# A fused retention and mixture-of-experts kernel: where the closing additions of each batch are done

## The chip, the cores and the metric

The kernel runs on one core of a Trainium2 chip. The metric is the device time of one execution in microseconds (us), taken as the median of several runs. The core's engines work side by side, each through its own queue in order: PE (matrix products), DVE (vector), ACT (scalar functions), POOL (general), and SP, whose queue issues the DMA transfers.

## The reference, cut to what matters

Linear attention with decay gives 3072 tokens of 512 features (4 batches of 768), and a mixture of 4 experts is applied to each token, in float32:

```
for t in range(768):
    state = gamma * state + outer(k[t], v[t])
    y[t] = scale * q[t] @ state
x = y as (3072, 512)
p = domain_probs / sum(domain_probs)
out = sum over e of p[:, e] * (relu(x @ w1[e]) @ w2[e])      # w1[e]: 512 x 1024, w2[e]: 1024 x 512
```

## The kernel before, in words

**Seven products.** Both layers use Winograd's form of Strassen's scheme: a product of 2 x 2 blocks is made of seven products of blocks, numbered 1 to 7, and some additions. Each float32 operand is split in a high and a low part (`oh` and `ol` for the hidden values, `oh` by a copy on ACT, `ol` by a subtraction), and each product is three matrix products. One product of one half is six matmuls of 128 x 384.

**Rounds, steps, passes.** The hidden width is done in rounds of 256 columns, 16 rounds per batch (NRND), 64 in all. A round has seven steps (SEQ), each one product of layer 1 (p1, L483). The first batch uses another form of layer 2 (p2). From batch 1 on, layer 2 works on groups of two rounds, eight groups per batch (NP): each step does one unit of the group before, so that a group has 14 units, U0 to U13 below. `UNITS` (L43) gives their order: products 1, 3, 6, 7, 5, 4, 2, each for the half d = 0 and then d = 1 of 128 output columns. After the last round only units are left, 14 of them: the tail.

**A unit** (L553) multiplies into one of two PSUM banks, `ps_u`. In a batch's first group ACT copies the result to a tile `sum` in SBUF; afterwards DVE adds it to that tile (L420). The next unit but one needs the bank again, so PE cannot start it before this addition is done.

**Closing a batch.** After a unit of the eighth group, `finish` (L573) puts the last additions of Winograd's scheme, between tiles `sum` (L578), and the stores of the four result blocks (L584) on a list, `soon`, each with a wait: an entry with wait w is issued w + 1 passes later. `pass_step` (L477) runs once ahead of each step, 14 passes to a group. The order in which a queue gets its instructions is thus the order of the code and of these waits; an engine does not skip ahead. Before, POOL does most of the closing sums and DVE two per half, 3 + 6 and 3 + 5.

**Beside it** run, through the same queues: in each round, DVE's evacuations of layer 1 (`ps_y`, `ps_c`, `ps_z`, L420, and the gated values `b`, L454), four subtractions of POOL on `b` (L456, three together and one for product 4), ACT's copies `oh` (L442) and the subtractions `ol` (L447), on POOL for products 5, 7, 6 and 4, on DVE for 1, 3 and 2; and in the next batch's attention the products `ps_s` on PE and `sp` on DVE (L142), and the scaling of `kv` on POOL (L127). Batch 3 is the last, so there is no attention beside the closing of batch 2, nor beside the tail.

**Weights** of layer 1 are fetched four steps ahead (five buffers), those of layer 2 two pairs of units ahead (`v2`, three buffers, L323), all on SP's queue, which also issues the stores.

Of the kernel before, what the change touches and what calls it, by code (L numbers as in the profile page):

```python
# [12 lines left out]
B, H, S, D = 4, 8, 768, 64  # L13
# [12 lines left out]
NP = NRND // 2  # L26
# [14 lines left out]


UNITS = tuple((i, d) for i in (1, 3, 6, 7, 5, 4, 2) for d in range(2))  # L43
A2_AT = {1: 0, 2: 2, 4: 3, 6: 4, 7: 5, 3: 6, 5: 7}
LO_POOL = (5, 7, 6, 4)

# [4 lines left out]
def retention_moe(ctx: ExitStack, tc: tile.TileContext, qk, kv, w1, w2, probs, probt, cmask, cqs, cks, cys, out, out_t):  # L51
    nc = tc.nc
# [21 lines left out]
    def open_pool(name, bufs):  # L74
        npool[name] = sc_n.enter_context(tc.tile_pool(name=name, bufs=bufs, reuse_waits="tile"))
# [231 lines left out]

    wp1, wp2 = {}, {}

    def fetch_w1(g):  # L310

        n, k = divmod(g, 7)
        if NRND <= n < NRND * B:
            i = SEQ[k]
            wp1[n, i] = v1_p.tile([128, 2, 256], F32R, tag="v1", name="v1")
            nc.sync.dma_start(out=wp1[n, i].bitcast(F32), in_=kept1[n % NRND][:, A_AT[i]])

    def fetch_w2(g):
        q, k = divmod(g, 7)
        if q < NP * B:  # L320
            i = UNITS[2 * k][0]
            wp2[q, i] = npool["v2"].tile([128, 2, 2, 256], F32R, tag="v2", name="v2")
            nc.sync.dma_start(out=wp2[q, i].bitcast(F32), in_=kept2[q % NP][:, A2_AT[i]])  # L323

# [92 lines left out]
    def add(ps, u, o=None):  # L417

        o = ps if o is None else o
        nc.vector.tensor_tensor(out=o, in0=ps, in1=u, op=ALU.add)  # L420
        return o
# [129 lines left out]
    outs = []  # L551

    def unit(q, k):  # L553
        i, d = UNITS[k]
        b, qb = divmod(q, NP)
        w = wp2[q, i]
        ps = ps_o.tile([128, 512], F32, tag="o", name="ps_u")[:, 0:HB]
        ds = slice(128 * d, 128 * d + 128)
        m = 0
        for r in range(2):  # L560
            hi, lo, _ = op[2 * q + r, i]
            for l, o in ((0, hi), (0, lo), (1, hi)):
                nc.tensor.matmul(ps, lhsT=w[:, r, l, ds], rhs=o, start=(m == 0), stop=(m == 5))  # L563
                m += 1
        if qb == 0:
            psum[b, i, d] = npool["s"].tile([128, HB], F32, tag="ps", name="sum")
            nc.scalar.activation(out=psum[b, i, d], in_=ps, func=ACTF.Copy)
        else:
            add(ps, psum[b, i, d], psum[b, i, d])
        if qb == NP - 1:  # L570
            finish(b, i, d)

    def finish(b, i, d):  # L573
        p = {j: psum[b, j, d] for j in range(1, 8)}
        e1, e2 = nc.gpsimd, nc.vector

        def sums(wait, e, o, x):
            soon.append((wait, lambda: e.tensor_tensor(out=p[o], in0=p[o], in1=p[x], op=ALU.add)))  # L578

        def store(wait, j, f, h):  # L580

            rows = out_t[256 * f + 128 * d:256 * f + 128 * d + 128]
            to = rows[:, (b - 1) * S + HB * h:(b - 1) * S + HB * h + HB]
            soon.append((wait, lambda: nc.sync.dma_start(out=to, in_=p[j])))  # L584

        if i == 1:
            sums(0, e1, 2, 1)
        elif i == 6:
            sums(0, e1, 6, 1)
            sums(2, e2, 3, 6)  # L590
        elif i == 7:
            sums(0, e1, 7, 6)
            sums(1, e1, 4, 7)
        elif i == 5:
            sums(0, e1, 7, 5)
            sums(0, e2, 3, 5)
            store(2, 7, 1, 1)
            store(2, 3, 0, 1)
        elif i == 4:
            store(1, 4, 1, 0)  # L600
        elif i == 2:
            store(0, 2, 0, 0)


    def att_steps(b):
        ci0 = b * NCHB
        load_qk(ci0 + 1)
        for ci in range(ci0, ci0 + NCHB):
            old = ci > ci0
            last = ci == ci0 + NCHB - 1  # L610
            decay(ci)
            scale_v(ci)
            scores(ci)
            yield
            if old:
                values(ci - 1, not last)
                if ci - 1 >= ci0 + 3:
                    combine_x(b, ci - 1 - ci0 - 3, nc.vector, nc.gpsimd)
                load_qk(ci + 1)
            else:  # L620
                state(ci)()
            load_kv(ci + 1)
            yield
        values(ci, False)
        yield
        combine_x(b, 2, nc.vector, nc.gpsimd)
        yield

    with tc.manual_schedule():
# [65 lines left out]
        for n in range(NRND * B):  # L695
            g, r = divmod(n, NRND)
            if r == 0 and g + 1 < B:
                steps = att_steps(g + 1)
                due = -1.0
            if n == NRND:  # L700
                sc_a.close()
                open_pool("g", 2)
                open_pool("b", 6)
                fetch_gate(n)
            tiles = [3, 4, 5, 0, 1, 2] if 0 < n <= NRND else []
            q, first = divmod(n, 2)
            for k, i in enumerate(SEQ if n else FIRST):
                t = 7 * n + k
                fetch_w1(t + 4)
                pass_step()  # L710
                if n == NRND and k == 3:
                    for x in tiles:
                        p2(n - 1, x)
                    tiles = []
                    sc_b.close()
                    open_pool("op", 15)
                    open_pool("s", 14)
                    open_pool("v2", 3)
                if n > NRND and r % RPE == 0 and k == 0:
                    fetch_gate(n)  # L720
                s14 = 7 * first + k
                if n >= NRND and q == NRND // 2 and s14 == 10:
                    fetch_w2(7 * q)
                    fetch_w2(7 * q + 1)
                p1(n, i)
                if n > NRND + 1:
                    if s14 % 2 == 0:
                        fetch_w2(7 * (q - 1) + s14 // 2 + 2)
                    unit(q - 1, s14)
                elif k and tiles:  # L730
                    for _ in range(2 if n == NRND else 1):
                        p2(n - 1, tiles.pop(0))
                if r == NRND - 1 and g + 1 < B:
                    x_hi(g + 1, i)
                    e = nc.gpsimd if k in XPOOL else nc.vector
                    soon.append((XLATE[k] - 1 if g else 0, lambda b=g + 1, i=i, e=e: x_lo(b, i, eng=e)))
                if n < NRND:
                    weights(n, k)
                if n == NRND and k == 0:
                    save_w2(n - 1, wc2, 4)  # L740
                due += ATT_STEPS / 13 / 7
                while due >= 1 - 1e-6:
                    due -= 1
                    next(steps, None)
        q = NP * B - 1
# [64 lines left out]
```

## Time and profile before

| | |
|---|---|
| median of 3 runs (lowest, highest) | 1091.43 us (1091.34, 1093.07) |
| profiled execution, its own time | 1093.62 us |
| its span, first to last instruction | 1090.7 us |
| PE busy | 1050.8 us, 96% |
| DVE busy | 724.4 us, 66% |
| POOL busy | 679.6 us, 62% |
| ACT busy | 378.3 us, 35% |

The profile is of one execution. A line of its timeline gives start, length, engine, line of the code, operation, output <- inputs, and in brackets how long the engine had been idle and what ended that. Rows with x2 or more are merged, and their length is that of the whole. The length of an instruction can hold a wait for a port. The windows view gives busy time per engine in a stretch and the clock granted to PE, 1.00 being full speed.

### The profile page before, as it was taken

To read this page: it belongs to the slowest core of one execution; us is meant where nothing else is said; L and a number is where in the kernel's file an instruction comes from. 1 tells how busy PE (TensorE), PEld (TensorE's weight loads), DVE (VectorE), ACT (ScalarE), POOL (GpSimd) and SP (SyncE) were. 2 spreads that over 40 slices of the span, in tenths; PEclk is the share of its full clock that TensorE was granted. 3 is DMA by queue.
4 is the path that set the end of the run, shared out by engine and by line. 5 is a ranking of instruction groups with operands and counts; after the bars stand their busy time and mean duration, and the time that the engine had idled before them with its cause. 6 is when DMAs were issued, how large, how long until landed. Compare 5 with 4: busy or idle time off the path is not lost.

```text
span 1090.7 us, 18579 instructions
## 1 busy us (share of the span) xinstructions
PE 1050.8 (96%) x6696; PEld 993.4 (91%) x6696; DVE 724.4 (66%) x1214; ACT 378.3 (35%) x737; POOL 679.6 (62%) x645
## 2 busy tenths in 40 slices
PE   6689999999999999999999899999999899999996
PEld 5578888888878999999999899999999899999995
DVE  5857666676766476676688556667669546666665
ACT  2343433444443423223252432332233343333330
POOL 3566666666626656556579655656668865555557
PEclk9899999999999999999999999999999999999999
DMA  8479999999898888878786987877788788888875
GB/s 323 145 261 312 345 308 312 300 347 310 285 303 291 262 268 265 277 258 271 242 260 219 331 279 238 272 266 257 233 256 261 254 270 253 261 262 256 265 223 168
DMA packets 154603, 293.70 MB, mean 269 GB/s; under 512 B 12688, under 2 KB 77328, under 8 KB 154512
## 3 DMA queue, kind: packets, MB, share of 16 engines
q1 hardware_dynamic: 153792, 291.66, 81.9%
q8 instruction: 53, 0.87, 0.3%
q10 hardware_dynamic: 720, 0.86, 0.2%
q14 instruction: 38, 0.31, 0.1%
HBM read 223.22 MB, written 69.26 MB: 268 GB/s over the span
## 4 chain that ended last, share of the span: by engine, by line
PE 81%; DVE 7%; POOL 5%; DMA 3%; issue 2%; ACT 1%; SPq 0%; ACTq 0%; DVEq 0%; POOLq 0%
PE ps_u L563 28%; PE ps_x L502 22%; PE ps_o L537 11%; PE ps_z L502 11%; PE ps_y L502 5%; POOL b L456 2%; POOL sum L578 2%; PE ps_s L139 2%; PE ps_v L186 2%; DVE xl L240 2%; DVE ol L447 1%; POOL ol L447 1%; PE ps_v L180 1%; DMA w2r<-in_w 1%; DMA v<-k 1%
## 5 line engine op out<-in xcount | busy, mean ns | idle before, releaser
L563 PE MATMUL ps_u<-oh,v 128*128 128x384 f32 x1344 | 395.5, 336 | 8.5 <-DVE sum L420 8.5
L456 POOL TENSOR_TENSOR b<-b 128x384 f32<-128x384 f32 x192 | 206.7, 1076 | 179.0 <-DVE b L454 147.5
L563 PEld LDWEIGHTS ps_u<-oh,v 128*128 128x128 f32 x1344 | 247.8, 188 | 12.2 <-DVE sum L420 12.0
L447 POOL TENSOR_TENSOR ol<-b,oh 128x384 fp32r<-128x384 f32 x192 | 207.8, 1094 | 81.1 <-ACT oh L442 43.5
L420 DVE TENSOR_TENSOR sum<-ps_u,sum 128x384 f32<-128x384 f32 x294 | 161.7, 550 | 136.4 <-PE ps_u L563 129.0
L442 ACT ACTIVATE oh<-b 128x384 fp32r<-128x384 f32 x336 | 163.1, 520 | 214.5 <-POOL b L456 123.8
L502 PE MATMUL ps_x<-xh,v 128*128 128x384 f32 x768 | 227.2, 336 | 1.3 <-ACT u L414 1.3
L563 PE MATMUL ps_u<-ol,v 128*128 128x384 f32 x672 | 225.0, 335 | 1.3 <-POOL ol L447 1.3
L414 ACT ACTIVATE u<-ps_x 128x384 f32<-128x384 f32 x128 | 62.6, 489 | 238.5 <-PE ps_x L502 238.4
L502 PEld LDWEIGHTS ps_x<-xh,v 128*128 128x128 f32 x768 | 141.4, 188 | 3.4 <-ACT u L414 1.6
L447 DVE TENSOR_TENSOR ol<-b,oh 128x384 fp32r<-128x384 f32 x144 | 127.9, 888 | 22.2 <-ACT oh L442 22.1
L502 PE MATMUL ps_x<-xl,v 128*128 128x384 f32 x384 | 128.4, 334 | 0.0
L563 PEld LDWEIGHTS ps_u<-ol,v 128*128 128x128 f32 x672 | 126.3, 188 | 1.7 <-POOL ol L447 1.7
L502 PE MATMUL ps_z<-xh,v 128*128 128x384 f32 x384 | 115.0, 340 | 2.4 <-DMA v<-k 2.4
L545 DVE SCALAR_TENSOR_TENSOR acc<-ps_o,pm,acc 128x512 f32<-128x512 f32 x90 | 67.0, 745 | 54.9 <-PE ps_o L537 54.9
L537 PE MATMUL ps_o<-w2l,hh 128*128 128x512 f32 x192 | 76.6, 399 | 0.0
L537 PE MATMUL ps_o<-w2h,hh 128*128 128x512 f32 x192 | 76.5, 398 | 0.2
L537 PE MATMUL ps_o<-w2h,hl 128*128 128x512 f32 x192 | 76.5, 398 | 0.0
L502 PEld LDWEIGHTS ps_z<-xh,v 128*128 128x128 f32 x384 | 71.6, 190 | 3.8 <-DVE c2l L290 2.7
L502 PEld LDWEIGHTS ps_x<-xl,v 128*128 128x128 f32 x384 | 72.1, 188 | 0.1
L502 PE MATMUL ps_z<-xl,v 128*128 128x384 f32 x192 | 64.8, 338 | 0.0
L420 DVE TENSOR_TENSOR ps_y<-ps_y,u 128x384 f32<-128x384 f32 x64 | 36.0, 563 | 33.6 <-PE ps_y L502 33.6
(109 smaller groups left out, 1630.5 us busy)
## 6 DMA issues: line engine op xcount, KB each, us to landing
v<-k SPq DMA_DIRECT2D x336, 256.0 KB, 3.8
v<-k SPq DMA_DIRECT2D x168, 512.0 KB, 4.5
k<-w1h SPq DMA_DIRECT2D x16, 896.0 KB, 6.3
k<-w1l SPq DMA_DIRECT2D x16, 896.0 KB, 8.4
qk<-in_qk SPq DMA_DIRECT2D x24, 512.0 KB, 5.5
kv<-in_kv SPq DMA_DIRECT2D x23, 512.0 KB, 5.8
w1r<-in_w SPq DMA_DIRECT2D x16, 512.0 KB, 7.9
w2r<-in_w SPq DMA_DIRECT2D x16, 512.0 KB, 4.3
```

Source lines behind the costliest of these rows:

```text
L139: nc.tensor.matmul(ps[r][:, p, :], lhsT=a[rows, 1, p, :], rhs=a[rows, 0, p, :], start=True, stop=True)
L186: nc.tensor.matmul(ps[r][64 * k:64 * k + 64, half, :], lhsT=v[:, 1, h, :], rhs=sp[:, h, :], start=(c == 0 and half == 0), stop=True, skip_ ...
L240: eng.tensor_tensor(out=lo, in0=x_part(b, i, o), in1=hi.bitcast(F32), op=ALU.subtract)
L414: nc.scalar.activation(out=t, in_=ps, func=ACTF.Copy)
L420: nc.vector.tensor_tensor(out=o, in0=ps, in1=u, op=ALU.add)
L442: nc.scalar.activation(out=hi, in_=t, func=ACTF.Copy)
L447: eng.tensor_tensor(out=lo, in0=t, in1=hi.bitcast(F32), op=ALU.subtract)
L456: sub = lambda o, a, b: nc.gpsimd.tensor_tensor(out=o, in0=a, in1=b, op=ALU.subtract)
L502: nc.tensor.matmul(ps, lhsT=lhsT[:, cs], rhs=rhs[:, kt, :], start=(fresh and m == 0), stop=(m == 5), skip_group_check=True,)
L537: nc.tensor.matmul(ps, lhsT=a[:, ts], rhs=b[:, fs, :], start=(m == 0), stop=(m == 5))
L545: nc.vector.scalar_tensor_tensor(out=acc[nt], in0=ps, scalar=sc, in1=acc[nt], op0=ALU.mult, op1=ALU.add)
L563: nc.tensor.matmul(ps, lhsT=w[:, r, l, ds], rhs=o, start=(m == 0), stop=(m == 5))
```

## The change

Three things change. In batches 1 and 2 the closing sums get longer waits, and product 4's sum (4 + 7) goes from POOL to DVE and now follows the unit's own addition instead of preceding it; the last block is built as 5 + 7 in the tile of product 5 (before: 7 + 5, after 4 had taken 7). The stores move to later passes. In the tail (the closing of batch 3) the units have another order, products 1, 3, 5, 7, 6, 4, 2, and all sums of half 0 are on POOL, all of half 1 on DVE. The pool of `sum` tiles grows from 14 to 16 buffers.

```diff
+LAST_UNITS = tuple((i, d) for i in (1, 3, 5, 7, 6, 4, 2) for d in range(2))
...
+    def units(q):
+        return LAST_UNITS if q == NP * B - 1 else UNITS
...
     def finish(b, i, d):
         p = {j: psum[b, j, d] for j in range(1, 8)}
-        e1, e2 = nc.gpsimd, nc.vector
+        pool, dve = nc.gpsimd, nc.vector
...
-        if i == 1:
-            sums(0, e1, 2, 1)
+        if b == B - 1:
+            e = (pool, dve)[d]
+            if i == 1:
+                sums(1, e, 2, 1)
+            elif i == 5:
+                sums(1, e, 3, 5)
+            elif i == 6:
+                sums(0, e, 6, 1)
+                sums(0, e, 7, 6)
+                sums(0, e, 3, 6)
+                store(0, 3, 0, 1)
+                sums(0, e, 5, 7)
+                store(0, 5, 1, 1)
+            elif i == 4:
+                sums(0, e, 4, 7)
+                store(0, 4, 1, 0)
+            elif i == 2:
+                store(0, 2, 0, 0)
+        elif i == 1:
+            sums(4, pool, 2, 1)
         elif i == 6:
-            sums(0, e1, 6, 1)
-            sums(2, e2, 3, 6)
+            sums(1, pool, 6, 1)
+            sums(4, dve, 3, 6)
         elif i == 7:
-            sums(0, e1, 7, 6)
-            sums(1, e1, 4, 7)
+            sums(1, pool, 7, 6)
         elif i == 5:
-            sums(0, e1, 7, 5)
-            sums(0, e2, 3, 5)
-            store(2, 7, 1, 1)
-            store(2, 3, 0, 1)
+            sums(1, dve, 3, 5)
+            store(3, 3, 0, 1)
+            sums(3, pool, 5, 7)
+            store(5, 5, 1, 1)
         elif i == 4:
-            store(1, 4, 1, 0)
+            sums(2, dve, 4, 7)
+            store(4, 4, 1, 0)
         elif i == 2:
-            store(0, 2, 0, 0)
+            store(1, 2, 0, 0)
...
-                    open_pool("s", 14)
+                    open_pool("s", 16)
```

In the orders below the numbers of the tiles tell them apart. POOL at the closing of batch 1, from the first sum on product 7 on; product 7's sums are 3707 and 3730 (halves 0 and 1), product 6's 3648 and 3673, product 5's 3759 and 3787, product 4's 3811 and 3838. Before:

```order
L578 TENSOR_TENSOR sum_3707<-sum_3707,sum_3648 128x384
L447 TENSOR_TENSOR ol_6450<-b_6337,oh_6449 128x384
L578 TENSOR_TENSOR sum_3811<-sum_3811,sum_3707 128x384
L578 TENSOR_TENSOR sum_3730<-sum_3730,sum_3673 128x384
L447 TENSOR_TENSOR ol_6481<-b_6391,oh_6480 128x384
L447 TENSOR_TENSOR ol_6484<-b_6364,oh_6483 128x384
L578 TENSOR_TENSOR sum_3838<-sum_3838,sum_3730 128x384
L578 TENSOR_TENSOR sum_3707<-sum_3707,sum_3759 128x384
L456 TENSOR_TENSOR b_6411<-b_6411,b_6364 128x384
L578 TENSOR_TENSOR sum_3730<-sum_3730,sum_3787 128x384
L447 TENSOR_TENSOR ol_6536<-b_6411,oh_6535 128x384
L127 TENSOR_TENSOR kv_5526<-kv_5526,ks_113 128x512
```

The same stretch in the change:

```order
L582 TENSOR_TENSOR sum_3673<-sum_3673,sum_3567 128x384
L451 TENSOR_TENSOR ol_6448<-b_6335,oh_6447 128x384
L582 TENSOR_TENSOR sum_3707<-sum_3707,sum_3648 128x384
L451 TENSOR_TENSOR ol_6478<-b_6389,oh_6477 128x384
L451 TENSOR_TENSOR ol_6481<-b_6362,oh_6480 128x384
L582 TENSOR_TENSOR sum_3730<-sum_3730,sum_3673 128x384
L460 TENSOR_TENSOR b_6410<-b_6410,b_6362 128x384
L451 TENSOR_TENSOR ol_6531<-b_6410,oh_6530 128x384
L582 TENSOR_TENSOR sum_3759<-sum_3759,sum_3707 128x384
L128 TENSOR_TENSOR kv_5526<-kv_5526,ks_113 128x512
L582 TENSOR_TENSOR sum_3787<-sum_3787,sum_3730 128x384
```

Ahead of the single subtraction (b_6411, now b_6410) three sums have gone from this queue: the two of product 4 and the first with product 5, which now comes after it.

DVE at the end of the same closing, from the addition of U10 (sum_3811, product 4, half 0) on; sum_3880 and sum_3900 are U12 and U13. Before:

```order
L420 TENSOR_TENSOR sum_3811<-ps_u_6525,sum_3811 128x384
L420 TENSOR_TENSOR ps_c_6549<-ps_x_6430,u_6466 128x384
L454 SCALAR_TENSOR_TENSOR b_6551<-ps_c_6549,g_6246 128x384
L420 TENSOR_TENSOR sum_3838<-ps_u_6553,sum_3838 128x384
L447 TENSOR_TENSOR ol_6541<-b_6521,oh_6540 128x384
L420 TENSOR_TENSOR ps_z_6459<-ps_z_6459,u_6498 128x384
L454 SCALAR_TENSOR_TENSOR b_6578<-ps_z_6459,g_6246 128x384
L420 TENSOR_TENSOR sum_3880<-ps_u_6582,sum_3880 128x384
L142 TENSOR_TENSOR sp_6593<-ps_s_6594,mask_111 128x4x128
L447 TENSOR_TENSOR ol_6569<-b_6551,oh_6568 128x384
L454 SCALAR_TENSOR_TENSOR b_6617<-ps_x_6430,g_6246 128x384
L420 TENSOR_TENSOR sum_3900<-ps_u_6619,sum_3900 128x384
```

The change, from the sum that now follows U10's addition (the second sp is left out here as above):

```order
L582 TENSOR_TENSOR sum_3619<-sum_3619,sum_3787 128x384
L424 TENSOR_TENSOR ps_c_6543<-ps_x_6428,u_6462 128x384
L458 SCALAR_TENSOR_TENSOR b_6545<-ps_c_6543,g_6246 128x384
L424 TENSOR_TENSOR sum_3838<-ps_u_6547,sum_3838 128x384
L451 TENSOR_TENSOR ol_6535<-b_6516,oh_6534 128x384
L424 TENSOR_TENSOR ps_z_6455<-ps_z_6455,u_6493 128x384
L458 SCALAR_TENSOR_TENSOR b_6571<-ps_z_6455,g_6246 128x384
L424 TENSOR_TENSOR sum_3880<-ps_u_6575,sum_3880 128x384
L582 TENSOR_TENSOR sum_3811<-sum_3811,sum_3707 128x384
L451 TENSOR_TENSOR ol_6562<-b_6545,oh_6561 128x384
L458 SCALAR_TENSOR_TENSOR b_6611<-ps_x_6428,g_6246 128x384
L424 TENSOR_TENSOR sum_3900<-ps_u_6613,sum_3900 128x384
```

One of DVE's sums now stands behind U10's addition, and one (4 + 7) between the additions of U12 and U13. The three sums ahead of U10's (3 + 6 twice, 3 + 5) stand behind the additions of U8 and U9; before, all four stood between the additions of U6 and of U10.

DVE in the tail; product 6, half 1 is sum_9875, and product 4's halves are sum_10001 and sum_10028. Before, from the addition of U5 on:

```order
L420 TENSOR_TENSOR sum_9875<-ps_u_12212,sum_9875 128x384
L420 TENSOR_TENSOR sum_9897<-ps_u_12223,sum_9897 128x384
L578 TENSOR_TENSOR sum_9799<-sum_9799,sum_9850 128x384
L420 TENSOR_TENSOR sum_9920<-ps_u_12233,sum_9920 128x384
L578 TENSOR_TENSOR sum_9821<-sum_9821,sum_9875 128x384
L420 TENSOR_TENSOR sum_9949<-ps_u_12246,sum_9949 128x384
L578 TENSOR_TENSOR sum_9799<-sum_9799,sum_9949 128x384
L420 TENSOR_TENSOR sum_9977<-ps_u_12257,sum_9977 128x384
L578 TENSOR_TENSOR sum_9821<-sum_9821,sum_9977 128x384
L420 TENSOR_TENSOR sum_10001<-ps_u_12267,sum_10001 128x384
```

The change, from the addition of U9 (product 6, half 1) to the end:

```order
L424 TENSOR_TENSOR sum_9875<-ps_u_12255,sum_9875 128x384
L582 TENSOR_TENSOR sum_9875<-sum_9875,sum_9768 128x384
L582 TENSOR_TENSOR sum_9920<-sum_9920,sum_9875 128x384
L582 TENSOR_TENSOR sum_9821<-sum_9821,sum_9875 128x384
L582 TENSOR_TENSOR sum_9977<-sum_9977,sum_9920 128x384
L424 TENSOR_TENSOR sum_10001<-ps_u_12269,sum_10001 128x384
L424 TENSOR_TENSOR sum_10028<-ps_u_12279,sum_10028 128x384
L582 TENSOR_TENSOR sum_10028<-sum_10028,sum_9920 128x384
L424 TENSOR_TENSOR sum_10055<-ps_u_12289,sum_10055 128x384
L424 TENSOR_TENSOR sum_10075<-ps_u_12298,sum_10075 128x384
```

Four sums in a row now stand between the additions of U9 and U10, where before sums and additions alternated. POOL has five sums of half 0 in a row from the unit of product 6 on, besides 2 + 1 and 3 + 5 earlier.

More of the change, by code (lines that the diff above doesn't have):

```diff
@@ L320, in fetch_w2 @@
         if q < NP * B:
-            i = UNITS[2 * k][0]
+            i = units(q)[2 * k][0]
             wp2[q, i] = npool["v2"].tile([128, 2, 2, 256], F32R, tag="v2", name="v2")
@@ L553, in unit @@
     def unit(q, k):
-        i, d = UNITS[k]
+        i, d = units(q)[k]
         b, qb = divmod(q, NP)
```

## The prediction

> **What bounds the kernel now.** Read first: the page, then the windows view (columns: microseconds; busy PE, weight loads, DVE, ACT, POOL; clock; DMA).
>
> ```profile
> span 1090.7 us, 18579 instructions
> 600.00:650.00 50.00, 46.95 (x311) 45.30 (x310) 28.40 (x50) 20.22 (x45) 29.66 (x29) 1.00 0.91 307
> 650.00:700.00 50.00, 50.00 (x342) 48.77 (x341) 34.06 (x61) 14.12 (x30) 29.91 (x30) 1.00 0.79 254
> 850.00:900.00 50.00, 46.52 (x257) 45.88 (x257) 23.53 (x39) 20.63 (x46) 33.87 (x34) 0.97 0.80 265
> ```
>
> In the steady stretch PE is never idle. It idles where a batch closes: batch 1 around 600 us, batch 2 around 858, and in the tail. The timeline of PE has the gaps, in brackets with what ended them:
>
> ```profile
> 584.32 0.44 PE L563 MATMUL ps_u<-oh,v 128*128 128x384 f32 x1 [0.22 <-DVE sum L420]
> 602.79 0.44 PE L563 MATMUL ps_u<-oh,v 128*128 128x384 f32 x1 [2.31 <-DVE sum L420]
> 605.91 0.44 PE L563 MATMUL ps_u<-oh,v 128*128 128x384 f32 x1 [0.74 <-DVE sum L420]
> 842.42 0.44 PE L563 MATMUL ps_u<-oh,v 128*128 128x384 f32 x1 [0.21 <-DVE sum L420]
> 855.85 0.44 PE L563 MATMUL ps_u<-oh,v 128*128 128x384 f32 x1 [0.65 <-DVE sum L420]
> 861.06 0.51 PE L563 MATMUL ps_u<-oh,v 128*128 128x384 f32 x1 [2.83 <-DVE sum L420]
> 1072.12 0.45 PE L563 MATMUL ps_u<-ol,v 128*128 128x384 f32 x1 [1.34 <-POOL ol L447]
> 1078.51 0.44 PE L563 MATMUL ps_u<-oh,v 128*128 128x384 f32 x1 [1.59 <-DVE sum L420]
> ```
>
> Batch 1 loses 0.22 + 2.31 + 0.74 = 3.27 us, batch 2 loses 0.21 + 0.65 + 2.83 = 3.69. Nearly always a unit waits for the addition that empties the PSUM bank of the unit two before it. Batch 2 pays more: after the gap the clock is low.
>
> ```profile
> 861.00:865.00 4.00, 3.94 (x14) 3.94 (x15) 2.48 (x5) 1.31 (x3) 3.70 (x4) 0.57 0.95 264
> 318.21 0.41 PE L502 MATMUL ps_z<-xh,v 128*128 128x384 f32 x1 [2.41 <-DMA v<-k]
> 320.00:324.00 4.00, 4.00 (x15) 3.26 (x14) 1.26 (x3) 0.49 (x1) 0.00 (x0) 0.75 1.01 365
> 864.81 0.34 PE L563 MATMUL ps_u<-oh,v 128*128 128x384 f32 x1
> 1066.78 0.56 DVE L420 TENSOR_TENSOR sum<-ps_u,sum 128x384 f32<-128x384 f32 x1 [0.48 <-PE ps_u L563]
> 1067.82 0.56 DVE L420 TENSOR_TENSOR sum<-ps_u,sum 128x384 f32<-128x384 f32 x1 [0.48 <-PE ps_u L563]
> ```
>
> Undisturbed, a group of six matmuls takes 1.04 us: so far apart are the additions of the tail's first units, at 1066.78 and 1067.82, each waiting for PE. From 861.06 to 864.81 two groups take 3.75 us instead of 2.08: 1.67 more, so batch 2 costs 5.36. A gap of 2.41 us was followed by a low clock too, the one of 2.31 was not (clock 1.00 in the first window above).
>
> Why is the addition late? The rows around 600 us, on POOL, ACT and DVE:
>
> ```profile
> 595.93 1.95 POOL L578 TENSOR_TENSOR sum<-sum 128x384 f32<-128x384 f32 x2
> 597.84 0.99 POOL L456 TENSOR_TENSOR b<-b 128x384 f32<-128x384 f32 x1
> 598.87 1.35 ACT L442 ACTIVATE oh<-b 128x384 fp32r<-128x384 f32 x3 [8.77 <-POOL b L456]
> 596.95 0.56 DVE L420 TENSOR_TENSOR sum<-ps_u,sum 128x384 f32<-128x384 f32 x1 [2.18 <-POOL sum L578]
> 599.84 1.36 DVE L447 TENSOR_TENSOR ol<-b,oh 128x384 fp32r<-128x384 f32 x1 [2.34 <-ACT oh L442]
> 602.19 0.55 DVE L420 TENSOR_TENSOR sum<-ps_u,sum 128x384 f32<-128x384 f32 x1
> ```
>
> POOL's closing sums hold up its subtraction b (product 4 of the round before); ACT, in order, waits 8.77 us for it; DVE waits 2.18 us for a POOL sum, then 2.34 us for ACT; the addition of U12 ends at 602.74, and the next group's first unit starts at 602.79.
>
> **The change part by part: batches 1 and 2.** POOL loses the sums of product 4 and takes two for product 5 in place of the two on product 7. Of the old nine sums ahead of that subtraction six stay.
>
> ```profile
> L578 POOL TENSOR_TENSOR sum<-sum x30: 987/1026/1733, 573.9 to 1083.6; 128x384 f32<-128x384 f32 x30
> L578 DVE TENSOR_TENSOR sum<-sum x12: 547/890/1415, 585.6 to 1081.0; 128x384 f32<-128x384 f32 x12
> ```
>
> Three times 1.03 us brings its end from 598.83 to 595.7, and ACT's two copies (about 1.0) free DVE's ol at 596.7. The additions of products 4 no longer wait for POOL, since 4 + 7 now follows them on DVE: the 2.18 us wait goes. What is late next is DVE itself. In its new order, between the addition of U8 and that of U13, stand eight operations with two SBUF inputs (five sums, three ol), twelve that read PSUM, and the two sp. Their cadence:
>
> ```profile
> 592.09 0.55 DVE L420 TENSOR_TENSOR ps_y<-ps_y,u 128x384 f32<-128x384 f32 x1
> 594.21 0.56 DVE L454 SCALAR_TENSOR_TENSOR b<-ps_c,g 128x384 f32<-128x384 f32 x1
> 602.65 1.27 DVE L142 TENSOR_TENSOR sp<-ps_s,mask 128x512 f32<-128x512 f32 x2
> 586.53 0.33 PE L563 MATMUL ps_u<-oh,v 128*128 128x384 f32 x1
> 599.27 0.33 PE L502 MATMUL ps_x<-xh,v 128*128 128x384 f32 x1
> ```
>
> Four PSUM readers take 2.12 us from start to start, 0.53 each. U8 began at 586.53; without the gap of 0.22 and its slow restart (0.12) it begins at 586.19, and its addition is over at 587.9. With x for an operation with two SBUF inputs, the addition of U13 ends at 587.9 + 12 x 0.53 + 1.27 + 8x = 595.5 + 8x. The second unit of the next group needs it: from 599.27, less 0.34, plus 1.04 for the layer-1 product in between and 2.08 for one step, it is due at 602.05. So PE waits 8x - 6.5 us. x lies between 0.55 (alone) and 1.42; I take 1.0, somewhat above the median of the sums, 0.89, as POOL is busy throughout. The wait is 1.5 us, against 3.27: a gain of 1.8. At 0.55 nothing is left to wait for, a gain of 3.3; at 1.35 the wait is 4.3, a loss of 1.0. Here ol would start, at x = 1.0, at 587.9 + 5 + 7 x 0.53 = 596.6, just as POOL and ACT allow.
>
> Batch 2 has neither the sp on DVE nor the attention's matmuls on PE, which weigh alike (1.27 us, and 1.3: from 586.53 to 599.27 PE does eleven groups of 1.04 and these), so again 1.5 us, and no low clock: 5.36 - 1.5, a gain of 3.9 (5.4 down to -0.6).
>
> The stores go to later passes on SP's queue, past loads of weights that in before were issued behind them:
>
> ```profile
> 597.90 0.81 SPq L584 DMA_DIRECT2D out<-sum  x2
> ```
>
> The first store of batch 1 is issued at 597.90, just after POOL's sums at 595.93, and holds back the loads behind it; still none of the gaps above is ended by a DMA, as weights of layer 1 are fetched four steps (8.3 us) ahead. With sums ready about when their stores come up this gets easier, and it costs nothing; if a sum is late, the same 8.3 us cover it. Two more buffers of sums cover the later stores: nothing.
>
> **The tail.** Order 1, 3, 5, 7, 6, 4, 2: the units of 5 and 7 come before those of 6, as POOL makes their ol first, so the gap of 1.34 goes. Then one engine sums each half, both at once. That they hinder each other shows at 574 us, where DVE does two such operations in a row beside POOL:
>
> ```profile
> 573.94 1.73 POOL L578 TENSOR_TENSOR sum<-sum 128x384 f32<-128x384 f32 x1
> 573.50 1.30 DVE L240 TENSOR_TENSOR xl<-xr,xh 128x768 fp32r<-128x768 f32 x1
> 574.72 1.36 DVE L447 TENSOR_TENSOR ol<-b,oh 128x384 fp32r<-128x384 f32 x1
> 1075.61 9.03 POOL L578 TENSOR_TENSOR sum<-sum 128x384 f32<-128x384 f32 x8
> 1079.76 0.78 DVE L578 TENSOR_TENSOR sum<-sum 128x384 f32<-128x384 f32 x1
> 1081.05 0.78 DVE L578 TENSOR_TENSOR sum<-sum 128x384 f32<-128x384 f32 x1
> 1083.70 3.95 SPq L584 DMA_DIRECT2D out<-sum  x8
> v<-k SPq DMA_DIRECT2D x6, 512.0 KB, 3.9
> ```
>
> POOL's sum takes 1.73 instead of 1.03, ends at 575.67, and DVE's ol, started at 574.72, ends 0.41 later: they take turns. In the old tail DVE's sums beside POOL's ended 1.29 us apart. The Trainium skill, SBUF — State Buffer, section "SBUF: two separate sides", says so: VectorE and GpSimd share a port pair under an exclusive lock, held for an instruction, and a VectorE operation with two SBUF inputs needs it. By that rule the sums of the two halves queue up, as in the rows; without it four sums of DVE would take 4 x 0.55.
>
> The unit k of the tail has its addition due at 1066.78 + 1.04k. U9's ends at 1076.7, or 1077.0: weights are fetched four units (about 4.0 us) ahead here and land after 3.9, so I allow 0.3 (0 to 0.6). Now DVE has four sums in a row before it may empty U10: 0.7 for the first (0.4 of its own and some of POOL's turn) and then three turns of 1.29, 4.6 us, to 1081.6. U10's addition (0.55) lets U12 start at 1082.2, where 1078.3 was due (its addition's time less 1.24, plus the 0.3), and U11 ended at 1078.5. After a gap of 3.7 us the clock will be low, as after 2.41 and 2.83: two units take 3.75 us, their last matmul 0.2 more, the last addition 0.6, and the last store is issued at 1086.75. In before the last of eight stores, 0.49 us apart, was issued at about 1087.2 and the span ended 3.5 us later. So 1090.2 for 1090.7: a gain of 0.5; at full clock 2.1.
>
> The sum is 1.8 + 3.9 + 0.5 = 6.2 us off a profiled execution of 1093.62 (span 1090.7). That execution was 2.2 slower than the median of the runs, 1091.43, in what the change doesn't touch, so I take the gain from the median: about 1085.3.
>
> **The rivals.**
> - The tail is clear: DVE gets the four sums in at 0.55 each, U12 starts at 1079.8, the clock stays, and the span ends at 1086.2, a gain of 4.5. With 5.7 from the batches: 1081.2. For it: the old tail's additions stood between DVE's sums, so four in a row there are not shown. Against it: the rows at 574.
> - POOL stays the limiter: DVE's five sums per closing make POOL's operations longer, as the 1.73 does, and its subtraction ends at 597.8 instead of 595.7. Then ol starts at 598.8, the wait is 3.7 in each batch, batch 1 loses 0.4, batch 2 gains 1.7, the tail 0.5: 1089.6, within the noise. Against it: three sums less.
> - Slower: DVE becomes the bound of the closings. From x = 1.1 the single gap before the second unit passes 2.3 us, and the clock drops (1.67 us) in batch 1 as well; at 1.35, near the upper end, batch 1 costs 4.3 + 1.67, batch 2 the same: 11.9 against 8.63, and with nothing from the tail 1094.7. For it: operations in a row each wait for POOL's turn. Against it: the old closing had the same contention and a median of 0.89.
>
> On the clock there is a rule too. The Trainium skill, TensorE: Matmul & The Clock Gate, section "Why this matters for your kernels", sets about 3 us of idleness as the limit; by it a wait of 2.5 would be free of the drop, while this trace shows one after 2.41, so the row decides.
>
> **How the numbers follow.** Forecast 0.55, clear tail 0.16, POOL as limiter 0.18, slower 0.11. The range is 1080.5 to 1090.5: from the clear tail to just over the POOL case, with x between 0.85 and 1.2. A measurement of this kernel can tell about 0.2%, 2.2 us, from no change. Faster by more: 0.55 + 0.16 + 0.07 of the POOL case = 0.78; the same: 0.14; slower by more: 0.08, most of the slower rival.
>
> **What would show it.** Right: at both closings no wait of DVE for a POOL sum, the subtraction about 3 us earlier, one gap of 1 to 2 us before the second unit of the next group and none of 2.8, the clock 1.00 after batch 2; in the tail one gap of 3 to 4 us before U12 behind four slow DVE sums, and stores that no longer end in a row of eight. Wrong: gaps before U11 or U12 within a closing, DVE's sums above 1.2 us on average, a wait for weights in the tail of over 1 us, or a tail without a gap.

## The result, and the profile after

The changed kernel took 1083.67 us, median of five runs (1080.76 to 1085.64), against 1091.34 us, median of five runs of the kernel before on the same chip: ratio 0.9931, 95% interval 0.9909 to 0.9952, 7.7 us less. Measured again later, it came to 1083.50 (five runs) against 1091.70: 0.9926, 0.9912 to 0.9940. The profiled execution is the fastest of the first five, 1080.76 us. Its span, 1078.9 us, is 11.8 us shorter than that of before, but 3.5 us of this lie ahead of the first changed instruction (the first unit of batch 1's eighth group starts at 565.77, before at 569.26), so the two profiles are compared stretch by stretch.

The page of the changed kernel, its windows (columns as before), and its timeline of PE with all gaps left at the closings and in the tail:

```profile
span 1078.9 us, 18574 instructions
...
PE 1048.2 (97%) x6696; PEld 991.3 (92%) x6696; DVE 731.2 (68%) x1221; ACT 378.7 (35%) x737; POOL 673.0 (62%) x638
```

```profile
854.00:858.00 4.00, 3.36 (x19) 3.36 (x20) 2.49 (x4) 2.60 (x6) 3.11 (x4) 1.00 0.96 322
1072.00:1074.00 2.00, 1.66 (x9) 1.66 (x10) 1.97 (x4) 0.00 (x0) 1.01 (x1) 0.93 0.83 295
1074.00:1076.00 2.00, 1.43 (x5) 0.93 (x3) 0.86 (x2) 0.00 (x0) 0.00 (x0) 0.50 0.83 298
```

```profile
582.53 0.33 PE L567 MATMUL ps_u<-oh,v 128*128 128x384 f32 x1
...
599.70 0.44 PE L567 MATMUL ps_u<-oh,v 128*128 128x384 f32 x1 [1.01 <-DVE sum L424]
851.32 0.44 PE L567 MATMUL ps_u<-oh,v 128*128 128x384 f32 x1 [0.34 <-DVE sum L424]
854.64 0.44 PE L567 MATMUL ps_u<-oh,v 128*128 128x384 f32 x1 [0.94 <-DVE sum L424]
1060.00 0.41 PE L567 MATMUL ps_u<-oh,v 128*128 128x384 f32 x1 [0.18 <-DMA v<-k]
1072.34 0.44 PE L567 MATMUL ps_u<-oh,v 128*128 128x384 f32 x1 [3.14 <-DVE sum L424]
```

The first row is U8 of batch 1's closing, the point from which times are counted below (586.53 before). Batch 1 loses 1.01 us instead of 3.27; batch 2 loses 0.34 + 0.94 = 1.28 instead of 3.69, and its clock stays at 1.00, where 0.57 stood before. The tail has one long gap, 3.14, in place of 1.34 + 1.59, and the clock is low in its last 2 us. From U0 of the closing to the layer-1 product behind the second unit of the next group, batch 1 takes 35.10 us instead of 37.80, batch 2 34.59 instead of 38.47; the tail, from its first unit to the end of the span, 23.43 instead of 25.16. Together that is 8.3 us, the rest of the 11.8; the medians show 7.7.

POOL and ACT at the closing of batch 1, in the changed kernel:

```profile
576.33 3.27 POOL L582 TENSOR_TENSOR sum<-sum 128x384 f32<-128x384 f32 x3
579.55 3.51 POOL L460 TENSOR_TENSOR b<-b 128x384 f32<-128x384 f32 x3
...
588.82 1.33 POOL L582 TENSOR_TENSOR sum<-sum 128x384 f32<-128x384 f32 x1
590.12 1.00 POOL L460 TENSOR_TENSOR b<-b 128x384 f32<-128x384 f32 x1
591.16 0.94 ACT L446 ACTIVATE oh<-b 128x384 fp32r<-128x384 f32 x2 [5.80 <-POOL b L460]
```

POOL's single subtraction ends at 591.12, 8.59 us after the start of U8; before it ended 12.30 after it (598.83 less 586.53). DVE behind U8's addition, the same closing:

```profile
584.24 1.18 DVE L582 TENSOR_TENSOR sum<-sum 128x384 f32<-128x384 f32 x1
585.34 1.36 DVE L451 TENSOR_TENSOR ol<-b,oh 128x384 fp32r<-128x384 f32 x1
...
587.10 2.18 DVE L582 TENSOR_TENSOR sum<-sum 128x384 f32<-128x384 f32 x2
...
592.99 1.15 DVE L451 TENSOR_TENSOR ol<-b,oh 128x384 fp32r<-128x384 f32 x1
...
596.86 0.57 DVE L582 TENSOR_TENSOR sum<-sum 128x384 f32<-128x384 f32 x1
597.35 1.36 DVE L451 TENSOR_TENSOR ol<-b,oh 128x384 fp32r<-128x384 f32 x1
...
599.10 0.54 DVE L424 TENSOR_TENSOR sum<-ps_u,sum 128x384 f32<-128x384 f32 x1
```

No row from 584.24 to the end of U13's addition at 599.64 has a bracket: DVE does not wait for another engine's result here, and its own row of operations is the limit. Their lengths hold turns with POOL, as the experiments show. The tail, DVE, POOL, and the stores on SP's queue:

```profile
1067.44 4.38 DVE L582 TENSOR_TENSOR sum<-sum 128x384 f32<-128x384 f32 x4
1071.74 1.01 DVE L424 TENSOR_TENSOR sum<-ps_u,sum 128x384 f32<-128x384 f32 x2
1066.43 4.97 POOL L582 TENSOR_TENSOR sum<-sum 128x384 f32<-128x384 f32 x4 [0.58 <-DVE sum L424]
1070.16 6.23 SPq L588 DMA_DIRECT2D out<-sum  x8
```

The four sums in a row take 4.38 us beside POOL's, and only then DVE empties the bank that U12 needs.

### The profile page after: what moved, and what is told of

Its sections match the earlier page's. It is cut to its first block, busy times and chain, and to the rows that moved or that the text cites. A ratio compares the mean times of both kernels' runs of the same rounds, so it can differ in the third digit from the quotient of the medians.

```text
span 1078.9 us, 18574 instructions
## 1 busy us (share of the span) xinstructions
PE 1048.2 (97%) x6696; PEld 991.3 (92%) x6696; DVE 731.2 (68%) x1221; ACT 378.7 (35%) x737; POOL 673.0 (62%) x638
## 4 chain that ended last, share of the span: by engine, by line
PE 85%; DVE 8%; issue 3%; DMA 2%; POOL 1%; ACT 1%; ACTq 0%; SPq 0%; POOLq 0%; DVEq 0%
PE ps_u L567 31%; PE ps_x L506 23%; PE ps_z L506 11%; PE ps_o L541 10%; PE ps_y L506 5%; PE ps_s L140 2%; PE ps_v L187 2%; DVE xl L241 1%; DVE sum L582 1%; DMA w2r<-in_w 1%; PE ps_v L181 1%; DVE ol L451 1%; DMA w1r<-in_w 1%; DVE sum L424 1%; DMA ks<-in_cks 1%
## 5 line engine op out<-in xcount | busy, mean ns | idle before, releaser
L451 POOL TENSOR_TENSOR ol<-b,oh 128x384 fp32r<-128x384 f32 x192 | 211.2, 1112 | 81.8 <-ACT oh L446 44.6
L451 DVE TENSOR_TENSOR ol<-b,oh 128x384 fp32r<-128x384 f32 x144 | 130.3, 905 | 15.3 <-ACT oh L446 15.3
L541 PE MATMUL ps_o<-w2h,hh 128*128 128x512 f32 x192 | 75.5, 393 | 0.3 <-DVE acc L549 0.2
```

Of the source, the lines that this page charges most:

```text
L451: eng.tensor_tensor(out=lo, in0=t, in1=hi.bitcast(F32), op=ALU.subtract)
L541: nc.tensor.matmul(ps, lhsT=a[:, ts], rhs=b[:, fs, :], start=(m == 0), stop=(m == 5))
```

## The experiments

Ratios are to the kernel before, run on the same chip beside each; a diff is against the changed kernel unless it says otherwise.

**The two halves of the change apart.** First the batches' closings alone, the tail as before:

```diff
-        return LAST_UNITS if q == NP * B - 1 else UNITS
+        return UNITS
...
         if b == B - 1:
-            e = (pool, dve)[d]
             if i == 1:
-                sums(1, e, 2, 1)
-            elif i == 5:
-                sums(1, e, 3, 5)
+                sums(0, pool, 2, 1)
             elif i == 6:
-                sums(0, e, 6, 1)
...
+                sums(0, pool, 6, 1)
+                sums(2, dve, 3, 6)
+            elif i == 7:
+                sums(0, pool, 7, 6)
+                sums(1, pool, 4, 7)
...
```

> The change in batches 1 and 2 alone; batch 3 closes in the old order with the old waits. My theory: the batches give most of the gain. The spans of the two profiles give 2.7 us less for the closing of batch 1 and 3.9 less for batch 2, so about 6.6 us faster than before, ratio 0.994, with one gap of about 1.0 us after batch 1, about 1.3 in two pieces after batch 2, and in the tail the old gaps of 1.34 and 1.59. Rival (the tail gives it): 2 us faster or less.

Measured: 1085.68 us, ratio 0.9947 (0.9935 to 0.9959), 5.6 us less than before by the medians, where 6.6 was expected. Gaps 1.01 in batch 1, 0.34 + 0.96 in batch 2, 1.13 and 1.59 in the tail.

Then the tail alone, with the closings of batches 1 and 2 as before:

```diff
         elif i == 1:
-            sums(4, pool, 2, 1)
+            sums(0, pool, 2, 1)
         elif i == 6:
-            sums(1, pool, 6, 1)
-            sums(4, dve, 3, 6)
+            sums(0, pool, 6, 1)
+            sums(2, dve, 3, 6)
         elif i == 7:
-            sums(1, pool, 7, 6)
+            sums(0, pool, 7, 6)
+            sums(1, pool, 4, 7)
...
```

> The change in the tail alone; batches 1 and 2 close as before. My theory: the tail is worth 1.7 us by the two profiles (23.4 us from its first unit to the end instead of 25.1), ratio 0.998 to 0.999, with one gap of about 3.1 us before U12, and the gaps of 2.3 and 2.8 after batches 1 and 2 back. Rival (the tail gives the gain): over 5 us faster.

Measured: 1091.09 us (12 runs), ratio 0.9997 (0.9984 to 1.0009). The new tail by itself changes nothing that can be measured; the batches alone bring 5.6 of the 7.7 us. Whether the 2 us between are noise, or the new tail is worth something beside the new closings, these intervals leave open. The gap before U12 is 3.44 us here, with a low clock from the restart on (timeline of PE, then the windows view):

```profile
1079.72 0.59 PE L567 MATMUL ps_u<-oh,v 128*128 128x384 f32 x1 [3.44 <-DVE sum L424]
```

```profile
1080.00:1082.00 2.00, 2.00 (x7) 2.00 (x7) 1.13 (x2) 0.00 (x0) 0.75 (x1) 0.50 0.84 301
```

**Do the tail's two rows of sums hinder each other?** The change without POOL's four sums of half 0 behind product 6 in the tail; half 0 of batch 3's output is then incomplete.

```diff
             elif i == 6:
-                sums(0, e, 6, 1)
-                sums(0, e, 7, 6)
-                sums(0, e, 3, 6)
+                if d:
+                    sums(0, e, 6, 1)
+                    sums(0, e, 7, 6)
+                    sums(0, e, 3, 6)
                 store(0, 3, 0, 1)
-                sums(0, e, 5, 7)
+                if d:
+                    sums(0, e, 5, 7)
```

> The change with POOL's four sums behind the unit of product 6, half 0, left out in the tail, so DVE's four sums in a row run with no POOL instruction beside them. If the two engines take turns at a shared port: the four take about 2 us instead of 4.38, the gap before U12 falls from 3.1 to about 0.8, and the clock stays at 1.00 to the end. If DVE's sums are slow by themselves or wait for each other's results: 4.4 us and a gap of 3.1 as before.

One run, 1079.67 us, too few for a comparison of times. Its DVE and its PE in the tail:

```profile
1069.50 2.09 DVE L582 TENSOR_TENSOR sum<-sum 128x384 f32<-128x384 f32 x4
```

```profile
1072.12 0.44 PE L567 MATMUL ps_u<-oh,v 128*128 128x384 f32 x1 [1.16 <-DVE sum L424]
```

The same four sums take 2.09 us instead of 4.38: the other half is POOL's doing. The gap falls by 1.98, to 1.16, and the clock stays at 1.00.

**Does the tail's gap cost the tail its length?** The change, with the sums of half 1 in the tail one per pass between the additions:

```diff
-                sums(0, e, 7, 6)
-                sums(0, e, 3, 6)
-                store(0, 3, 0, 1)
-                sums(0, e, 5, 7)
-                store(0, 5, 1, 1)
+                sums(1 * d, e, 7, 6)
+                sums(2 * d, e, 3, 6)
+                store(2 * d, 3, 0, 1)
+                sums(3 * d, e, 5, 7)
+                store(3 * d, 5, 1, 1)
             elif i == 4:
-                sums(0, e, 4, 7)
-                store(0, 4, 1, 0)
+                sums(2 * d, e, 4, 7)
+                store(2 * d, 4, 1, 0)
```

> The change, with the tail's sums of half 1 on DVE one per pass instead of four in a row ahead of the emptying of U10; the batches' closings as in the change. Theory (the four in a row cost the tail a gap of 3.1 us and a low clock): the gap before U12 falls to below 0.5, the clock stays at 1.00, batch 1 keeps its gap of 1.0; time 2 to 3.5 us less than the change: 1080 to 1082, ratio 0.990 to 0.992. Rival (the tail's end is set by the stores and by DMA): the gap goes but the end doesn't move, 1083 to 1084.

Measured: 1083.77 us, ratio 0.9926 (0.9912 to 0.9939), the change's own. The gap before U12 is gone, and the end does not move; so the rival named there held, and the theory that the gap costs the tail its length fell. The timeline of this kernel's last matmul and its stores:

```profile
1072.54 0.34 PE L567 MATMUL ps_u<-oh,v 128*128 128x384 f32 x1
...
1071.93 5.73 SPq L588 DMA_DIRECT2D out<-sum  x8
```

PE is done at 1072.88, 7.7 us before the span ends at 1080.6; in the change 3.5 us (1075.44 of 1078.9). The eight stores begin when POOL's third sum is done, 1071.93; the second and third start at 1073.22 and 1074.49, each as POOL's next sum ends, the other five follow until 1077.66, when the units have long been done, and the span ends 2.9 later. In the change the last store waits for U13's addition instead (issued at 1076.06, the span ends 2.8 later). With the gap gone, a limit of nearly the same length, POOL's sums and the stores behind them, stands in its place.

**Which part of the batches' change counts?** First the new split (4 + 7 on DVE behind the unit, 5 + 7 on POOL) with the short waits of before:

```diff
         elif i == 1:
-            sums(4, pool, 2, 1)
+            sums(0, pool, 2, 1)
         elif i == 6:
-            sums(1, pool, 6, 1)
-            sums(4, dve, 3, 6)
+            sums(0, pool, 6, 1)
+            sums(2, dve, 3, 6)
         elif i == 7:
-            sums(1, pool, 7, 6)
+            sums(0, pool, 7, 6)
...
...
         elif i == 4:
-            sums(2, dve, 4, 7)
+            sums(0, dve, 4, 7)
...
```

> The other part alone: 4 + 7 on DVE after the unit of product 4, and 5 + 7 on POOL, but each sum and store with the short waits of before; the tail is the new one. Theory (the move frees POOL, the waits only smear the sums): POOL's subtraction stands behind six or seven sums, as with the change, no DVE wait for POOL, one gap of about 1.0 in batch 1 and a sum of 1.0 to 1.8 in batch 2, some 0.2 more at the first units: 1083.5 to 1085.5, ratio 0.993 to 0.995. Rival (the clump of sums is the trouble): gaps of over 2 us as before, time 1087 or more, ratio above 0.996.

Measured: 1087.02 us, ratio 0.9965 (0.9953 to 0.9977). The theory put on record fell, by the gaps most of all (timelines of PE, POOL, DVE):

```profile
587.02 0.34 PE L567 MATMUL ps_u<-oh,v 128*128 128x384 f32 x1
...
603.16 0.45 PE L567 MATMUL ps_u<-oh,v 128*128 128x384 f32 x1 [2.19 <-DVE sum L424]
606.29 0.45 PE L567 MATMUL ps_u<-oh,v 128*128 128x384 f32 x1 [0.77 <-DVE sum L424]
584.86 1.26 POOL L582 TENSOR_TENSOR sum<-sum 128x384 f32<-128x384 f32 x1 [0.81 <-DVE sum L424]
586.08 4.08 POOL L460 TENSOR_TENSOR b<-b 128x384 f32<-128x384 f32 x3
596.90 1.00 POOL L460 TENSOR_TENSOR b<-b 128x384 f32<-128x384 f32 x1
598.90 1.36 DVE L451 TENSOR_TENSOR ol<-b,oh 128x384 fp32r<-128x384 f32 x1 [3.23 <-ACT oh L446]
600.18 1.40 DVE L582 TENSOR_TENSOR sum<-sum 128x384 f32<-128x384 f32 x1
```

DVE's wait for a POOL sum is gone (2.18 before), but 0.9 of it comes back in the wait for ACT's oh, 3.23 instead of 2.34. POOL's subtraction still ends 10.88 us after U8 starts. With short waits a sum is on POOL's queue before the addition that it needs: POOL idles 0.81 us in front of it, and three subtractions queue behind. They start 0.94 us before U8 (0.97 in the kernel before), in the change 2.98 before it. Then the sum at 600.18 (1.32 us to the next start) stands ahead of U12's addition. Batch 1's gaps are 0.23 + 2.19 + 0.77, batch 2's 0.19 + 2.50 with a low clock behind. The median is still 4.3 us below before, while the two closings, over the stretches used above, take 37.69 + 37.18 us instead of 37.80 + 38.47: 1.4 less. The tail of this execution kept its clock at 1.00 and is 2.4 shorter than before; no run shows what the median owes to that.

The other part alone, the long waits, with 4 + 7 still on POOL ahead of the unit:

```diff
         elif i == 7:
             sums(1, pool, 7, 6)
+            sums(2, pool, 4, 7)
         elif i == 5:
             sums(1, dve, 3, 5)
             store(3, 3, 0, 1)
-            sums(3, pool, 5, 7)
-            store(5, 5, 1, 1)
+            sums(3, pool, 7, 5)
+            store(5, 7, 1, 1)
         elif i == 4:
-            sums(2, dve, 4, 7)
             store(4, 4, 1, 0)
```

> The change with one part of the closings of batches 1 and 2 undone: the sum 4 + 7 stays on POOL, ahead of the units of product 4, and 7 takes 5 (stored at the end of the passes) as before; all waits are the later ones, the tail is the new one. Theory (it is the move of 4 + 7 that frees DVE and POOL): the addition of U10 waits for POOL's sum again, about 0.9 us, POOL's subtraction stands behind one sum more, 1.0 to 1.3 us later, and ol may wait 0.4 for ACT; DVE has a sum less (0.5 to 1.0). The gap of batch 1 is 1.3 to 2, batch 2's sum 1.5 to 2.5: 1084 to 1086.5, ratio 0.993 to 0.996. Rival (the later waits are what helps, who does 4 + 7 is of no account): no wait of DVE for a POOL sum, a gap of 0.5 or less as DVE has less to do, time 1083 or less, ratio below 0.993.

Measured: 1083.01 us, ratio 0.9922 (0.9907 to 0.9937), the change's time without its new split. Timelines of PE, POOL and DVE:

```profile
585.05 0.34 PE L567 MATMUL ps_u<-oh,v 128*128 128x384 f32 x1
...
601.54 0.44 PE L567 MATMUL ps_u<-oh,v 128*128 128x384 f32 x1 [0.29 <-DVE sum L424]
851.35 0.44 PE L567 MATMUL ps_u<-oh,v 128*128 128x384 f32 x1 [0.65 <-DVE sum L424]
582.07 3.52 POOL L460 TENSOR_TENSOR b<-b 128x384 f32<-128x384 f32 x3
593.62 1.32 POOL L460 TENSOR_TENSOR b<-b 128x384 f32<-128x384 f32 x1
595.93 0.56 DVE L424 TENSOR_TENSOR sum<-ps_u,sum 128x384 f32<-128x384 f32 x1 [0.80 <-POOL sum L582]
```

The waits of the theory are there (0.80 us for a POOL sum, the subtraction's end 9.89 after U8, 1.3 later than in the change), but the gaps are smaller than in the change, 0.29 and 0.65, as DVE has two sums less. The theory's time, 1084 to 1086.5, fell; the rival's held, but not its sign that DVE would not wait for POOL. Over the same stretches the two closings take 34.44 + 33.87 = 68.3 us here, 69.7 in the change, 74.9 with the split alone and 76.3 before. So the long waits carry the gain, and the new split added to them costs the closings 1.4 us: it frees POOL by 1.3 us and loads DVE, which is the limiter by then.

One wait alone, as a check between the two: the kernel with the short waits, with DVE's 4 + 7 two passes later.

```diff
-            sums(0, dve, 4, 7)
-            store(2, 4, 1, 0)
+            sums(2, dve, 4, 7)
+            store(4, 4, 1, 0)
```

> The kernel with the new split and the short waits of before, with one wait lengthened: DVE's 4 + 7 and its store wait two passes longer, as in the change. Theory (what the long waits bring is that POOL's subtraction, ACT's oh and so DVE's first ol come earlier; the sums of 4 + 7 only move within DVE's chain): ol still starts about 11.9 us after U8, the gap before the first unit of the next group falls from 2.2 to about 0.9, the one before the second grows from 0.8 to about 1.9; sum near 2.8, time within 1 us of the kernel without this, 1086 to 1088. Rival (what the long waits bring is only that 4 + 7 no longer stands ahead of the addition of U12): sum of the gaps 1 to 1.5 per closing, time 1083 to 1085.

Measured: 1085.91 us, ratio 0.9946 (0.9933 to 0.9959). Batch 1's gaps are 0.19 + 0.62 + 1.21, sum 2.02, batch 2's 0.20 + 1.94 + 0.94, sum 3.08; ol starts 11.55 us after U8. In between: in batch 1 the sum of 4 + 7 ahead of U12's addition had cost 1.2 us, in batch 2 moving it took nothing off the gaps. Both effects of the long waits count, the earlier subtraction and the place of 4 + 7; how they share the rest stays open.

**Is DVE the limiter of the new closing?** The change, with one more DVE operation with two SBUF inputs per half and closing:

```diff
...
             sums(1, dve, 3, 5)
+            soon.append((1, lambda: nc.vector.tensor_tensor(out=extra, in0=p[6], in1=p[1], op=ALU.add)))
```

> The change, with one more DVE operation with two SBUF inputs per half at the closings of batches 1 and 2 (p6 + p1 into a tile that nobody reads), issued two passes after the unit of product 5: two more per closing, between the additions of U8 and U13. Theory (DVE is the limiter of a closing, PE waits 8x - 6.5 with x = 1.0): two more make it 10x, so the wait grows by 2.0 us per closing, from 1.01 to about 3.0 in batch 1 and from 1.28 to about 3.3 in batch 2, ended by DVE's additions; a single gap of 3.0 may bring a low clock, up to 1.7 us more each. Time 4 to 7.5 us over the change, 1087.5 to 1091. Rival (POOL and ACT's oh still set when the additions come): DVE has slack, and the gaps stay within 0.5 us of 1.01 and 1.28; time 1083 to 1085.

Measured: 1085.61 us, ratio 0.9955 (0.9939 to 0.9970), 2 us over the change. Timelines of DVE and PE:

```profile
590.89 1.36 DVE L619 TENSOR_TENSOR extra<-sum 128x384 f32<-128x384 f32 x1
594.16 1.37 DVE L619 TENSOR_TENSOR extra<-sum 128x384 f32<-128x384 f32 x1
...
593.84 0.44 PE L568 MATMUL ps_u<-oh,v 128*128 128x384 f32 x1 [1.13 <-DVE sum L425]
603.07 0.44 PE L568 MATMUL ps_u<-oh,v 128*128 128x384 f32 x1 [1.22 <-DVE sum L425]
```

Batch 1's gaps grow from 1.01 to 2.35, batch 2's from 1.28 to 2.98 (1.14 + 0.90 + 0.94). That is 0.7 to 0.85 us per operation, not the 1.0 of the expectation; the stretches grow by 1.7 and 1.9 us. The gaps came in pieces, none above 1.22, and the clock stayed at 1.00, so the time lies below the 1087.5 to 1091 that were expected. The rival, slack on DVE, is out.

**Better versions.** The spread tail with 4 + 7 on DVE three passes later, beyond the units that wait (this diff and the next are against the kernel with the spread tail):

```diff
-            sums(2, dve, 4, 7)
-            store(4, 4, 1, 0)
+            sums(5, dve, 4, 7)
+            store(7, 4, 1, 0)
```

> The change, with the sums of half 1 in the tail one to a pass instead of four in a row, and the sums 4 + 7 of batches 1 and 2 issued three passes later, behind the addition of U13. My theory, that DVE's order is what is left: no gap before U12 and none over 0.5 us after the batches, no low clock in the tail; tail 3 us shorter and 2 us off the batches, so some 5 us faster than the change and 12 to 13 faster than before, ratio 0.988. Rival (POOL is what is late): as fast as the change, 0.993.

Measured: 1080.39 us, ratio 0.9901 (0.9887 to 0.9914), no gap in batch 1, 0.31 in batch 2. That is short of the expected 0.988: in the profiles the two closings are 2.4 us shorter than in the change, but the tail 1.1 and not 3. Again, beside the change on one chip:

> The changed kernel itself, beside the three others on one chip: ratio to before 0.991 to 0.995 as at first, gaps of 1.0 in batch 1 and 0.3 + 0.95 in batch 2, about 3.1 to 3.4 before U12 of the tail.

> The version with the tail's sums of half 1 one per pass and 4 + 7 three passes later, again, beside the change: if its gain over the change is real, 2 to 3.5 us below it, ratio to before 0.988 to 0.991; if the difference was one of chips, within 1 us of the change.

The change 1083.50, 0.9926 (0.9912 to 0.9940); the spread version 1079.71, 0.9892 (0.9873 to 0.9911): 3.8 us less, the intervals apart. And with 4 + 7 on POOL, behind the unit:

```diff
-            sums(2, dve, 4, 7)
+            sums(2, pool, 4, 7)
```

> The version with the spread tail and, in batches 1 and 2, 4 + 7 on POOL instead of DVE, after the units of product 4 (same wait as in the change). Theory (DVE is the limiter of the closing, POOL has slack behind its subtraction): two operations fewer in DVE's chain, 6x - 6.5 is below nothing: no gap in batch 1, 0 to 0.35 in batch 2, time as the spread version, 1079 to 1082, ratio 0.988 to 0.991. Rival (POOL's two sums hold up its next three subtractions and through ACT's oh the next ol): a gap of over 0.5 us at the first steps of the next group or of the next round, 1082 to 1085.

Measured: 1080.79 us, ratio 0.9896 (0.9881 to 0.9911), no gap in batch 1, 0.31 in batch 2. Taking the two sums off DVE's chain, by time or by engine, is worth the same; POOL had room for them behind its subtraction.

## Why the prediction was right, and where it was not

The forecast was 6.1 us less, with 1.8 from batch 1, 3.9 from batch 2, 0.5 from the tail; the medians gave 7.7, the stretches 2.7, 3.9 and 1.7.

**Batch 1: right, with a gain 0.5 us too small.** The wait was to be 8x - 6.5, with x = 1.0. In the rows of the change the eight operations with two SBUF inputs take 8.09 us from start to start, x = 1.01. That is about twice the 0.52 that such an operation took with POOL's sums away (2.09 for four), so about half of the 8 us is turns with POOL, an estimate from these two figures. They, the two sp (1.20) and the twelve readers of PSUM (6.11, 0.51 each and not 0.53) fill the 15.40 us from 584.24 to 599.64. The rest of the difference lies on PE: the second unit of the next group was due 16.16 us after U8 (599.70 - 1.01 - 582.53), not 15.86. So the gap was 1.0, not 1.5.

**Batch 2: the wait right, the 3.9 in part luck.** The wait was 1.28 instead of 1.5, split over two units, with no low clock; the stretch is 3.9 us shorter, as forecast. But 1.67 of the 3.9 stands for the low clock that followed the gap of 2.83 in the profile of before, and that is not fixed to this closing. In the profile of the tail alone, whose closings are the old ones, the clock stayed at 1.00 after batch 2's gap of 2.84 and fell after batch 1's of 2.50; there batch 1 takes 38.56 us and batch 2 36.92. The sum of the two is nearly the same, 75.5 and 76.3.

**The cause within the batches: the step "three sums fewer ahead of POOL's subtraction" came out in size, not in its origin.** It was to bring 3.1 us, and the subtraction came 3.7 earlier. The text put this down to sums that leave POOL's queue ahead of it, product 4's and one of product 5's. That move alone gives 12.30 - 10.88 = 1.4 us and leaves the gaps; the longer waits alone give 12.30 - 9.89 = 2.4 and take the gaps away. What the prediction passed over is that a sum that is queued before its unit's addition holds up POOL, and with it all that stands behind. It also counted on the end of DVE's 2.18 us wait; with the short waits it went, and the gaps stayed.

**The tail: the size right, the reason half.** The four sums took 4.38 us (forecast 4.6) and turned out 2.09 without POOL, so they do hinder each other. The gap was 3.14 to 3.45 (forecast 3.7), a low clock followed in six of seven executions, and alone the new tail gave a ratio of 0.9997. In the profile of the change the clock fell late, so U12 and U13 took 3.10 us (1072.34 to 1075.44) and not 3.75; with the shorter gap that makes about the 1.7 less that it shows for the tail. Two more terms were off and cancelled in part: U9 started 10.12 us after U0 (1065.59 less 1055.47) where 9 x 1.04 and the 0.3 make 9.66, and from the last store to the end of the span it took 2.8 us, not 3.5. But the chain of the forecast, gap, slow units, last store, is not what ends the tail alone: the version without the gap ends no earlier.

**The stores, costed at nothing,** cost nothing at the closings: no gap there is ended by a DMA. In the tail the wait for weights is 0.18 us in this profile and up to 0.56 in the others, within the 0 to 0.6 allowed.

**The rivals.** The clear tail is out: DVE's four sums took 4.38 beside POOL's, not 2.2. POOL as the limiter is out: no DVE operation of the closing waits for a result of POOL or ACT. The slower case needed x = 1.35 and met 1.01.

## What to carry to other kernels

When an engine takes its queue in order, an operation issued before its input is there costs not only its own wait but that of everything behind it; issue it later, where the input is surely ready, before moving it to another engine. After such a repair ask which engine is the limiter now, count its operations between two fixed points, and take off those that nobody waits for. A gap of the bound engine near the end is worth closing only if the stores behind it do not set the same end.

## What the runs showed of the hardware

The clock's answer to a gap depended on more than its length: low after 2.41, 2.50 and 2.83 us, at 1.00 after 2.84 (the tail alone, batch 2) and after 3.45 (the split alone, tail). In each of the 14 traces here all changes of the granted clock lie whole multiples of 3.41 us apart, on a grid that starts elsewhere in each execution. What counted was PE's idle time between two points of that grid. Two closings of the tail alone and the tail of the split alone (windows views on the grid; the number behind the comma is PE's busy time):

```profile
598.60:602.00 3.40, 1.03 (x6) 1.03 (x7) 3.37 (x6) 0.46 (x1) 3.01 (x4) 1.00 0.98 316
602.00:605.40 3.40, 3.40 (x12) 3.16 (x11) 2.60 (x5) 1.92 (x4) 2.84 (x3) 0.50 0.99 286
858.00:861.40 3.40, 1.55 (x9) 1.55 (x10) 3.37 (x7) 0.20 (x1) 1.85 (x2) 1.00 1.01 308
861.40:864.80 3.40, 3.40 (x21) 3.40 (x20) 1.15 (x2) 3.01 (x8) 3.20 (x4) 1.00 1.00 343
1079.80:1083.20 3.40, 1.67 (x9) 1.67 (x10) 3.37 (x5) 0.00 (x0) 1.81 (x2) 1.00 0.64 231
1083.20:1086.60 3.40, 0.69 (x4) 0.37 (x3) 0.87 (x2) 0.00 (x0) 0.00 (x0) 1.00 0.65 234
```

With 2.4 us idle in a window the next one is at 0.50; with 1.85 it is not, and the gap of 3.45 fell into two windows, 1.67 and 1.78 each. Of all windows after the first 60 us that began at full clock, every one with 2.0 us or more idle was followed by the low clock, none with less than 1.8 was, and near 1.86 both occur. So a gap between about 1.9 and twice that drops the clock or not by where it falls on the grid, which is chance; the prediction's line between 2.31 and 2.41 was no limit of its own.

The grid fits what the Trainium skill, TensorE: Matmul & The Clock Gate, section "What's actually happening", says of a free-running window of activity of about 3.4 us. That a whole window must be idle, as its table of states has it, does not fit: 2.4 of 3.4 us were enough.

POOL's and DVE's operations with SBUF inputs take turns. Two of those of the change's tail, one by one:

```profile
1068.83 1.30 POOL L582 TENSOR_TENSOR sum<-sum 128x384 f32<-128x384 f32 x1
1069.21 1.34 DVE L582 TENSOR_TENSOR sum<-sum 128x384 f32<-128x384 f32 x1
```

Behind DVE's first sum (0.56) three of POOL's and three of DVE's alternate: each of POOL's ends 0.85 us after DVE's, each of DVE's 0.42 after POOL's. A pair takes 1.27 us; alone, from start to start, DVE takes 0.52 and POOL 0.96 (two sums from 595.93 to 597.84 before, while DVE waits), together 1.48. So the turns are there, as the exclusive lock that the prediction cites from the Trainium skill would have them, but about 0.2 us of each pair overlaps, so whatever they take turns at is not held for the whole length that the profile shows.

The same code of the tail, spread, took 23.2 us from the last layer-1 product to the end in both executions with 4 + 7 late on DVE, and 24.4 in the two others. About 0.35 of the difference lies ahead of POOL's five sums, 0.3 in them and the rest in the stores; why is open.
